# Routing scores of the last three token tiles on TensorE instead of VectorE

## The chip, the core and the metric

The kernel runs on one core of a Trainium2 chip. A core has five engines that run their instruction streams in order and wait for one another through semaphores: TensorE (PE, matmuls and transposes into PSUM), VectorE (DVE), ScalarE (ACT), GpSimd (POOL) and SyncE (SP, which issues most of the transfers). The metric is the time of one execution on the device in microseconds (us). Timed runs of the kernel before took 796.22, 793.3 and 797.24 us, median 796.22.

## What is computed

Attention over 4 x 8 heads of 576 tokens, then a dense layer with a maximum over three projections, then a layer of eight experts in which each of the 2304 tokens goes to one expert. The last part is the one that the change touches:

```python
logits = x @ w_gate + modality_bias[modality_id]      # 2304 x 512 by 512 x 8
e_idx = np.argmax(logits, axis=1)
probs = np.exp(logits - logits.max(-1, keepdims=True))
probs /= probs.sum(-1, keepdims=True) + 1e-09
gate_w = probs[np.arange(N), e_idx]
for e in range(8):
    mask = e_idx == e
    h = np.maximum(x[mask] @ w1[e], 0.0)              # 512 -> 1024
    out[mask] = gate_w[mask, None] * (h @ w2[e])      # 1024 -> 512
```

All is float32 outside. Inside, most matmuls take each operand as a high and a low part (`h`/`l`, `hh`/`hl`, `e_h`/`e_l`), three matmuls for one product.

## The kernel before, in words

Attention fills the first 287 us or so. Then come six windows of 384 tokens, three token tiles of 128 each, 18 tiles in all (t = 0 to 17). For a window, `stage_a` makes the six blocks of the hidden layer, and for each tile `stage_b` makes 18 matmuls (L528 to L530, "b") into `b_ps`; ACT copies the sum to `x2` (L532), SP writes it to `x2d` (L533), and `route` finds the expert of each token of the tile.

`route` before: eight products with sums on DVE (L459), one per expert, each over 512 elements of the tile against gate weights that are held broadcast over the 128 partitions (`wg_sb`, four buffers of the pool `raw2`); the bias (L460), the maximum, the one-hot of the first maximum (L451 to L453); on PE two matmuls that give each token its rank within its expert (L467, L468, one PSUM bank `rk`); on ACT the exponential (L473); and a scatter of token number and weight into the table in DRAM (L482, issued by POOL).

Experts are worked in units of up to 256 tokens of one expert. Three units (0, 1, 2) are cut from the first 12 tiles and start before the routing is done; the other units are found by arithmetic on DVE over the final counts (L706 to L758, "the table arithmetic") after tile 17. For a unit, POOL gathers the rows of x2 (`xg`), PE transposes them (L580, `x_ps`), ACT and DVE split them (L581, L582), `stage_1` is its first layer (96 matmuls L597 to L599 into `h_ps`; ACT makes `gh` at L600, DVE `gl` at L601) and `stage_2` its second (two halves of 24 matmuls, L626 to L628). Expert weights come in loads of 512 KB (`e_raw`, L563); ACT casts each half of a load to `e_h` (L567), and DVE (first half) or POOL (second half) subtracts to `e_l` (L568).

Loads need a raw buffer: unit 0's eight loads alternate between the two buffers of `rawp`; from the ninth load (unit 1) on they alternate between `rawp` and the four buffers of `raw2`. The casts need buffers that dense-layer weights held until the last b matmuls read them. All of this is one program; a scheduler orders the instructions of each engine by its own estimate, so that an edit can shift the order of work that it does not name. Small PSUM tiles come from `ps_a` (five banks in rotation), `x2`-sized tiles in SBUF from `x2p` (three buffers).

Of the kernel before, what the change touches and what calls it, by code (L numbers as in the profile page):

```python
# [5 lines left out]
F32 = mybir.dt.float32  # L6
# [3 lines left out]
ALU = mybir.AluOpType  # L10
# [7 lines left out]
DM = H * D  # L18
FF1 = 768
NF1 = FF1 // 128  # L20
E, FF2 = 8, 1024
# [18 lines left out]
MW = 384  # L40
NW = T // MW
NT = T // 128
# [3 lines left out]
STRIDE = T + UNIT  # L46
T_EARLY = NT - 2 * (MW // 128)
N_EARLY = 3
NU_STATIC = 6
NU_MAX = 16  # L50
SENT = 1 << 20
# [27 lines left out]
CONV = {2: [0, 1], 3: [2], 4: [3, 4], 5: [5], 7: [6], 8: [7], 9: [8]}  # L79


def fused_kernel(tc, qk, vd, sd, w64, mod, wg, mb, we, cst, csi, out):
    nc = tc.nc
    V, A, G, P, SP = nc.vector, nc.scalar, nc.gpsimd, nc.tensor, nc.sync
    top = ExitStack()
    with top:
# [13 lines left out]
        ident = per.tile([128, 128], F32, name="ident")  # L100
# [5 lines left out]
        bias = per.tile([128, NT, E], F32, name="bias")  # L106
# [38 lines left out]
        with ExitStack() as es:  # L145
# [249 lines left out]
            for p in range(1, NP):  # L395
# [17 lines left out]
                if p % (H // 2) == H // 2 - 1:  # L413
                    b = p // (H // 2)
                    n = 0
# [12 lines left out]
        x2p = top.enter_context(tc.tile_pool(name="x2p", bufs=3, reuse_waits="tile"))  # L428
# [5 lines left out]
        unp = top.enter_context(tc.tile_pool(name="unp", bufs=1, reuse_waits="tile"))  # L434
# [7 lines left out]

        junk = jkp.tile([128, DM], BF16, name="junk")
        wg_sb = []

        def first_max(src, mx):

# [7 lines left out]

        def route(t, x2):
            lg = rp.tile([128, E], F32, name="lg")
            for ei in range(E):
                V.tensor_tensor_reduce(out=junk, in0=x2, in1=wg_sb[ei // 2][:, ei % 2, :], scale=1.0, scalar=0.0, op0=ALU.mult, op1=ALU.add, accum_out=lg[:, ei:ei + 1])  # L459
            V.tensor_tensor(out=lg, in0=lg, in1=bias[:, t, :], op=ALU.add)  # L460
            nm = rp.tile([128, 1], F32, name="nm")
            mx = rp.tile([128, 1], F32, name="mx")
            V.tensor_reduce(out=mx, in_=lg, axis=AX.X, op=ALU.max)
            oh, _ = first_max(lg, mx)

            rk = ps_r.tile([128, E], F32, name="rk")
            P.matmul(rk, tri, oh, start=True, stop=False)  # L467
            P.matmul(rk, ones, acc[:, t, :], start=False, stop=True)  # L468
            V.tensor_tensor(out=acc[:, t + 1, :], in0=acc[:, t, :], in1=oh, op=ALU.add)
            V.tensor_scalar(out=nm, in0=mx, scalar1=-1.0, scalar2=None, op0=ALU.mult)  # L470
            ex = rp.tile([128, E], F32, name="ex")
            sm = rp.tile([128, 1], F32, name="sm")
            A.activation(out=ex, in_=lg, func=ACTF.Exp, bias=nm, scale=1.0, accum_out=sm)  # L473
            V.tensor_scalar(out=sm, in0=sm, scalar1=1e-9, scalar2=None, op0=ALU.add)
            V.reciprocal(out=meta[:, t, 1:2], in_=sm)
            sl = rp.tile([128, E], F32, name="sl")
            s1 = rp.tile([128, 1], F32, name="s1")
            V.tensor_tensor(out=sl, in0=rk, in1=off, op=ALU.add)
            V.tensor_tensor_reduce(out=sl, in0=sl, in1=oh, scale=1.0, scalar=0.0, op0=ALU.mult, op1=ALU.add, accum_out=s1)
            si = rp.tile([128, 1], I32, name="si")  # L480
            V.tensor_copy(out=si, in_=s1)
            G.indirect_dma_start(out=table[:, :], out_offset=bass.IndirectOffsetOnAxis(ap=si[:, 0:1], axis=0), in_=meta[:, t, :], in_offset=None, bounds_check=TABLE - 1, oob_is_err=False)  # L482
# [322 lines left out]
def _layout(i):  # L805
    import numpy as np

    def heads(a):
# [19 lines left out]
    csi = (np.arange(NT)[None, :] * 128 + np.arange(128)[:, None]).astype(np.int32)  # L828
    return {
        "qk": qk, "vd": vd, "sd": s, "w64": w64, "mod": mod,  # L830
        "wg": i["moe2_w_gate"].T.reshape(1, E, DM), "mb": i["moe2_modality_bias"].reshape(1, 2, E),
        "we": np.concatenate([e1, e2], axis=1), "cst": cst, "csi": csi,
    }

# [18 lines left out]
```

## Time and profile before

| | |
|---|---|
| median of three runs | 796.22 us (793.3 to 797.24) |
| the profiled execution | 794.2 us |
| its span, first to last instruction | 792.1 us |
| PE busy | 722.5 us, 91% |
| DVE busy | 580.4 us, 73% |
| POOL busy | 391.5 us, 49% |
| ACT busy | 360.7 us, 46% |
| mean granted clock of PE | 0.974 of full speed |

The trace gives every instruction its engine, its line in the kernel (L459), the tiles it writes and reads, its start and its length, all in us from the start of the span. Idle time of an engine is put down to what released the instruction behind it. Matmuls overlap, so PE's busy time says that it is fed, and the distance from one matmul's start to the next says how fast it goes.

### The profile page before, as it was taken

The page shows a single profiled execution, that of the slowest core. Times are in us where ns is not written, and L with a number is a line of the kernel's source. Part 1 is how long each engine was busy: PE and PEld are TensorE (multiplying, and loading weights), DVE is VectorE, ACT ScalarE, POOL GpSimd, SP SyncE. Part 2 cuts the span into 40 slices and gives each one's busy share as a digit, 9 for nine tenths or more (in the row PEclk, how much of TensorE's full clock was granted, in tenths as well). Part 3 has the DMA queues.
Part 4 walks back from the last instruction along what each step waited for, and adds up shares of the span by engine and source line. Part 5 has one row for each costly group of instructions (what it writes and reads, how often), then busy time and mean ns, then how long its engine had stood idle before and what let it go on. Part 6 is the DMA issues. An engine that isn't in the chain of part 4 may idle for free. (4 is left out here: it accounts for less than half of the span.)

```text
span 792.1 us, 13768 instructions
## 1 busy us (share of the span) xinstructions
PE 722.5 (91%) x4530; PEld 640.3 (81%) x4530; DVE 580.4 (73%) x1523; ACT 360.7 (46%) x905; POOL 391.5 (49%) x413
## 2 busy tenths in 40 slices
PE   2687789988999995999999999989988999999996
PEld 1565678767989785999989899988877899998884
DVE  4687897869867657867889495994997687657740
ACT  3364556544656544422222221333364755656541
POOL 6544546453342044645253423357375876857640
PEclk9988999998999999999999999999999999999998
DMA  7977778788672145210120101336375867657520
GB/s 192 214 219 205 193 198 206 194 220 215 193 177 82 42 167 193 103 62 21 51 47 15 37 14 32 125 81 165 108 226 205 300 224 255 242 196 255 184 83 18
DMA packets 50561, 117.99 MB, mean 149 GB/s; under 512 B 10352, under 2 KB 14352, under 8 KB 50480
## 3 DMA queue, kind: packets, MB, share of 16 engines
q1 hardware_dynamic: 38072, 90.44, 37.2%
q0 software_dynamic: 12400, 26.57, 13.0%
q8 instruction: 38, 0.62, 0.4%
q14 instruction: 43, 0.35, 0.1%
q10 hardware_dynamic: 8, 0.01, 0.0%
HBM read 98.84 MB, written 12.18 MB: 140 GB/s over the span
## 5 line engine op out<-in xcount | busy, mean ns | idle before, releaser
L139 PE MATMUL a_ps<-xh,w_h 128*128 128x384 f32 (+2 forms) x492 | 159.9, 326 | 3.6 <-DVE h L318 3.0
L140 PE MATMUL a_ps<-xl,w_h 128*128 128x384 f32 (+2 forms) x492 | 159.6, 325 | 0.0
L141 PE MATMUL a_ps<-xh,w_l 128*128 128x384 f32 (+2 forms) x492 | 158.1, 322 | 0.0
L459 DVE CUSTOM_DVE_ANT_0 junk<-x,wg 128x512 bf16<-128x512 f32 x144 | 114.3, 794 | 36.5 <-ACT x L532 34.8
L241 ACT ACTIVATE e<-e,mn 128x64 f32<-128x64 f32 (+4 forms) x160 | 89.1, 558 | 84.1 <-DVE mn L239 83.7
L568 DVE TENSOR_TENSOR e_l<-e_raw,e_h 128x512 fp32r<-128x512 f32 x80 | 103.6, 1307 | 32.3 <-ACT e_h L567 29.2
L568 POOL TENSOR_TENSOR e_l<-e_raw,e_h 128x512 fp32r<-128x512 f32 x80 | 109.3, 1385 | 32.1 <-ACT e_h L567 26.0
L567 ACT CAST e_h<-e_raw 128x512 fp32r<-128x512 f32 x160 | 93.7, 621 | 52.5 <-DMA e_raw<-in_we 42.9
L139 PEld LDWEIGHTS a_ps<-xh,w_h 128*128 128x128 f32 x492 | 93.6, 191 | 5.6 <-DVE h L318 3.8
L140 PEld LDWEIGHTS a_ps<-xl,w_h 128*128 128x128 f32 x492 | 93.9, 191 | 0.9
L141 PEld LDWEIGHTS a_ps<-xh,w_l 128*128 128x128 f32 x492 | 93.7, 191 | 0.5
L237 PE MATMUL s_ps<-hl 128*128 128x64 f32 (+2 forms) x192 | 67.4, 363 | 23.4 <-DMA hl<-in_qk 10.4
L270 PE MATMUL t_ps<-ident,e 128*128 128x128 f32 x480 | 73.8, 290 | 9.1 <-DVE x L295 4.5
L598 PE MATMUL h_ps<-x2t,e_h 128*128 128x256 f32 x288 | 81.2, 283 | 0.0
L599 PE MATMUL h_ps<-x2t,e_l 128*128 128x256 f32 x288 | 80.9, 282 | 0.0
L597 PE MATMUL h_ps<-x2t,e_h 128*128 128x256 f32 x288 | 80.4, 284 | 0.3 <-DVE gl L601 0.3
L519 POOL TENSOR_TENSOR fl<-h,fh 128x384 fp32r<-128x384 f32 x36 | 42.9, 1197 | 73.8 <-ACT fh L518 55.4
L270 PEld LDWEIGHTS t_ps<-ident,e 128*128 128x128 f32 x480 | 59.8, 149 | 13.2 <-DVE x L295 4.9
L239 DVE CUSTOM_DVE_ANT_0 e<-s_ps,mask 128x64 f32<-128x64 f32 (+4 forms) x160 | 64.3, 424 | 8.1 <-PE s_ps L238 7.3
L238 PE MATMUL s_ps<-k_b,q_b 66*128 66x64 f32 (+2 forms) x192 | 61.0, 329 | 4.6 <-POOL q_b L209 4.6
L628 PE MATMUL y_ps<-e_h,gl 128*128 128x512 f32 x152 | 61.3, 403 | 3.0 <-DVE gl L601 3.0
L237 PEld LDWEIGHTS s_ps<-hl 128*128 128x128 f32 x192 | 39.7, 209 | 29.7 <-DVE mn L239 13.4
(174 smaller groups left out, 1576.7 us busy)
## 6 DMA issues: line engine op xcount, KB each, us to landing
e_raw<-in_we SPq DMA_DIRECT2D x80, 512.0 KB
w_raw<-in_w SPq DMA_DIRECT2D x24, 512.0 KB
qk_r<-in_qk SPq DMA_DIRECT2D x32, 288.0 KB
hl<-in_qk POOLq DMA_DIRECT2D x32, 288.0 KB, 4.9
v_r<-in_vd SPq DMA_DIRECT2D x16, 320.0 KB
rb<-r_d SPq DMA_DIRECT2D x32, 160.0 KB
hl<-in_qk POOLq DMA_DIRECT2D x32, 144.0 KB, 4.0
x2d<-x SPq DMA_DIRECT2D x18, 256.0 KB
```

The lines of the kernel that those rows point to most:

```text
L139: P.matmul(a_ps, wh[:, c], xh[:, c], start=c == 0, stop=False)
L140: P.matmul(a_ps, wh[:, c], xl[:, c], start=False, stop=False)
L141: P.matmul(a_ps, wl[:, c], xh[:, c], start=False, stop=c == 3)
L237: P.matmul(s_ps, hl[:, 1, q0:q0 + nq], hl[:, 0, k0:k0 + n], start=True, stop=False)
L241: ex = A.activation(out=ec, in_=ec, func=ACTF.Exp, bias=mn[0:nq, c:c + 1], scale=-1.0, accum_out=l[0:nq, c:c + 1]).ins
L270: last_t[0] = P.transpose(out=t_ps[:, n * 128:(n + 1) * 128], in_=e[:, EOFF[c] + kb * 128:EOFF[c] + (kb + 1) * 128], identity=ident).ins
L459: V.tensor_tensor_reduce(out=junk, in0=x2, in1=wg_sb[ei // 2][:, ei % 2, :], scale=1.0, scalar=0.0, op0=ALU.mult, op1=ALU.add, accum_out=l ...
L567: A.copy(out=h, in_=raw[:, a])
L568: (G if a else V).tensor_tensor(out=lo, in0=raw[:, a], in1=h.bitcast(F32), op=ALU.subtract)
L597: P.matmul(h_ps, w(hs, f, c), xt[:, 0, c], start=c == 0, stop=False)
L598: P.matmul(h_ps, w(hs, f, c), xt[:, 1, c], start=False, stop=False)
L599: P.matmul(h_ps, w(ls, f, c), xt[:, 0, c], start=False, stop=c == 3)
```

## The change

The gate weights are loaded a second time, in the layout that PE needs (`wgt`, 128 partitions of 4 x 8). For the last three tiles (`T_PE` is 15) `route` transposes x2 in four pieces on PE, ACT copies the result from PSUM, and four float32 matmuls of 8 columns give the scores in PSUM, which the addition of the bias reads there. Tiles 0 to 14 are routed as before.

```diff
+T_PE = NT - MW // 128
...
+        wgt_sb = unp.tile([128, 4, E], F32, name="wgt")
+        SP.dma_start(out=wgt_sb, in_=wgt)
...
             lg = rp.tile([128, E], F32, name="lg")
-            for ei in range(E):
+            src = lg
+            if t >= T_PE:
+
+                t_ps = ps_a.tile([128, 512], F32, tag="a", name="xt_ps")
+                for c in range(4):
+                    P.transpose(out=t_ps[:, c * 128:(c + 1) * 128], in_=x2[:, c * 128:(c + 1) * 128], identity=ident)
+                x2t = x2p.tile([128, DM], F32, tag="x2", name="x2t_r").rearrange("p (c n) -> p c n", c=4)
+                A.copy(out=x2t, in_=t_ps.rearrange("p (c n) -> p c n", c=4))
+                src = ps_a.tile([128, 512], F32, tag="a", name="lg_ps")[:, 0:E]
+                for c in range(4):
+                    P.matmul(src, x2t[:, c], wgt_sb[:, c], start=c == 0, stop=c == 3)
+            for ei in range(E if t < T_PE else 0):
                 V.tensor_tensor_reduce(out=junk, in0=x2, in1=wg_sb[ei // 2][:, ei % 2, :], scale=1.0, scalar=0.0, op0=ALU.mult, op1=ALU.add, accum_out=lg[:, ei:ei + 1])
-            V.tensor_tensor(out=lg, in0=lg, in1=bias[:, t, :], op=ALU.add)
+            V.tensor_tensor(out=lg, in0=src, in1=bias[:, t, :], op=ALU.add)
```

Up to the end of tile 15's matmuls the order on the engines is the old one, but for the load of `wgt`. From there on it moves. On PE before, from the end of tile 16's matmuls on; `x_ps` are unit 0's input transposes, the 18 matmuls of tile 17 begin with the row L528, and L597 opens unit 0's first layer:

```order
L580 MATMUL x_ps<-ident,xg 128x128 x2
L530 MATMUL b_ps<-w_h,fl_6275 128x512 x2
L580 MATMUL x_ps<-ident,xg 128x128 x6
L528 MATMUL b_ps<-w_h,fh_6039 128x512
...
L530 MATMUL b_ps<-w_h,fl_6275 128x512
L597 MATMUL h_ps<-x2t,e_h 128x256 x3
```

And now, with the lines of the changed kernel (L543 to L545 are b, L467 the new transposes, x_6395, x_6459 and x_6538 tiles 15, 16 and 17, L472 the new scores, L595 unit 0's transposes, L482 and L483 the ranks, L612 unit 0's first layer):

```order
L545 MATMUL b_ps<-w_h,fl_6277 128x512 x2
L467 MATMUL xt_ps<-ident,x_6395 128x128 x4
L543 MATMUL b_ps<-w_h,fh_6041 128x512
...
L545 MATMUL b_ps<-w_h,fl_6277 128x512
L472 MATMUL lg_ps<-wgt,x2t_r 128x8 x4
L467 MATMUL xt_ps<-ident,x_6459 128x128 x4
L472 MATMUL lg_ps<-wgt,x2t_r 128x8 x4
L595 MATMUL x_ps<-ident,xg 128x128 x8
L467 MATMUL xt_ps<-ident,x_6538 128x128 x4
...
L483 MATMUL rk<-acc,ones 128x8
L472 MATMUL lg_ps<-wgt,x2t_r 128x8 x4
L612 MATMUL h_ps<-x2t,e_h 128x256
```

Routing of all three tiles and unit 0's transposes moved between tile 17's matmuls and unit 0's first layer. On ACT before, from the copy of tile 15 on (L581 casts unit 0's transposed input, L600 is gh):

```order
L532 COPY x_6393<-b_ps 128x512
L532 COPY x_6453<-b_ps 128x512
L581 CAST x2t<-x_ps 128x512 x2
L567 CAST e_h<-e_raw 128x512
L532 COPY x_6528<-b_ps 128x512
L600 ACTIVATE gh<-h_ps 128x256 x4
```

And now (L547 copies x2, L469 the transposed x2, L582 is e_h, L488 the exponential, L596 unit 0's input):

```order
L547 COPY x_6395<-b_ps 128x512
L469 COPY x2t_r<-xt_ps 128x512
L547 COPY x_6459<-b_ps 128x512
L582 CAST e_h<-e_raw 128x512 x6
L469 COPY x2t_r<-xt_ps 128x512
L547 COPY x_6538<-b_ps 128x512
L488 ACTIVATE ex,sm<-lg,nm 128x8
L596 CAST x2t<-x_ps 128x512
L488 ACTIVATE ex,sm<-lg,nm 128x8
L596 CAST x2t<-x_ps 128x512
L469 COPY x2t_r<-xt_ps 128x512
```

Five more casts of expert weights stand ahead of the copy of the transposed tile 16. On SP before, the last three writes of x2 stood ahead of the tenth expert load:

```order
L563 DMA e_raw<-in_we 128x1024
L533 DMA x2d<-x_6393 128x512
L533 DMA x2d<-x_6453 128x512
L533 DMA x2d<-x_6528 128x512
L563 ISA
```

And now three more loads stand ahead of the first two of them (L548), and four behind those ahead of the third:

```order
L578 ISA
L578 DMA e_raw<-in_we 128x1024
L548 DMA x2d<-x_6395 128x512
L548 DMA x2d<-x_6459 128x512
L578 ISA
```

The loads moved ahead because the gate weights' buffers are free after tile 14.

## Rows read from the trace of the kernel before

**Rows 1.** Page, busy time: us, share of the span, instructions.
```profile
PE 722.5 (91%) x4530; PEld 640.3 (81%) x4530; DVE 580.4 (73%) x1523; ACT 360.7 (46%) x905; POOL 391.5 (49%) x413
```

**Rows 2.** PE by stage: stage, length, PE busy (count), granted clock, DMA share, GB/s.
```profile
551.38:562.74 11.36, 11.36 (x99) 1.00 0.17 57
562.74:574.73 11.99, 11.99 (x60) 1.00 0.62 194
574.73:590.80 16.07, 13.22 (x100) 0.89 0.80 249
590.80:608.20 17.40, 14.44 (x58) 0.90 0.39 138
608.20:620.50 12.30, 12.02 (x97) 1.00 0.87 323
```

**Rows 3.** Waits of PE, 551 to 610: total us, times, longest.
```profile
PE y_ps L628 <- DVE gl L601: 3.0, 3, 1.4
PE rk L467 <- DVE sm L474: 2.7, 1, 2.7
```

**Rows 4.** Timeline of PE, 574 to 584: start us, length us, instruction.
```profile
577.19 0.27 PE L599 MATMUL h_ps<-x2t,e_l 128*128 128x256 f32 x1
...
580.19 0.56 PE L597 MATMUL h_ps<-x2t,e_h 128*128 128x256 f32 x1
...
583.11 0.35 PE L599 MATMUL h_ps<-x2t,e_l 128*128 128x256 f32 x1
```

**Rows 5.** Lines of DVE, 545 to 575: busy us, mean ns; idle before.
```profile
L459 DVE CUSTOM_DVE_ANT_0 junk<-x,wg 128x512 bf16<-128x512 f32 x24 | 17.7, 739 | 4.5 <-ACT x L532 4.2
L459 DVE DVE_READ_ACCUMULATOR2_ANT lg<- 128x1 f32 x24 | 2.0, 82 | 0.0
```

**Rows 6.** Timelines of DVE and POOL, 571 to 599.
```profile
571.45 2.87 DVE L460 TENSOR_TENSOR lg<-lg,bias 128x8 f32<-128x8 f32 x1
...
598.10 0.41 DVE L601 SCALAR_TENSOR_TENSOR gl<-h_ps,gh 128x256 fp32r<-128x256 f32 x1
...
571.75 2.54 POOL L568 TENSOR_TENSOR e_l<-e_raw,e_h 128x512 fp32r<-128x512 f32 x2
...
596.54 2.78 POOL L568 TENSOR_TENSOR e_l<-e_raw,e_h 128x512 fp32r<-128x512 f32 x2 [2.34 <-DMA e_raw<-in_we]
```

**Rows 7.** Timeline of SP, 530 to 610: issues, merged, with their count.
```profile
532.30 3.33 SPq L563 DMA_DIRECT2D e_raw<-in_we  x2
547.14 5.37 SPq L533 DMA_DIRECT2D x2d<-x  x3
565.39 32.34 SPq L563 DMA_DIRECT2D e_raw<-in_we  x15
```

**Rows 8.** Transposes and float32 matmuls: two timeline rows, two groups of lines.
```profile
777.57 1.03 PE L616 MATMUL t_ps<-ident,h 128*128 128x128 f32 x8
...
287.04 0.29 PE L293 MATMUL t_ps<-pt,v_r 128*64 128x64 f32 x4
...
L293 PE MATMUL o_ps<-pt,v_r 128*64 128x512 f32 x64 | 18.2, 647 | 2.2 <-ACT pt L275 2.2
...
L293 PE MATMUL t_ps<-pt,v_r 128*64 128x64 f32 x64 | 4.6, 222 | 0.0
```

**Rows 9.** Timeline of ACT, 536 to 549.
```profile
536.35 0.62 ACT L567 CAST e_h<-e_raw 128x512 fp32r<-128x512 f32 x1 [2.50 <-DMA e_raw<-in_we]
...
541.61 0.62 ACT L567 CAST e_h<-e_raw 128x512 fp32r<-128x512 f32 x1 [3.73 <-DMA e_raw<-in_we]
...
546.53 1.08 ACT L532 COPY x<-b_ps 128x512 f32<-128x512 f32 x2 [3.89 <-PE b_ps L530]
547.49 1.10 ACT L581 CAST x2t<-x_ps 128x512 fp32r<-128x512 f32 x2
```

**Rows 10.** Timeline of DVE: two of the small routing operations.
```profile
564.61 0.15 DVE L463 TENSOR_REDUCE mx<-lg 128x1 f32<-128x8 f32 x1
...
565.28 0.23 DVE L451 TENSOR_SCALAR lt<-lg,mx 128x8 f32<-128x8 f32 x1
```

More of the change, by code (lines that the diff above doesn't have):

```diff
@@ L79, with fused_kernel @@
 CONV = {2: [0, 1], 3: [2], 4: [3, 4], 5: [5], 7: [6], 8: [7], 9: [8]}
-def fused_kernel(tc, qk, vd, sd, w64, mod, wg, mb, we, cst, csi, out):
+def fused_kernel(tc, qk, vd, sd, w64, mod, wg, wgt, mb, we, cst, csi, out):
     nc = tc.nc
@@ L830, in _layout @@
         "qk": qk, "vd": vd, "sd": s, "w64": w64, "mod": mod,
-        "wg": i["moe2_w_gate"].T.reshape(1, E, DM), "mb": i["moe2_modality_bias"].reshape(1, 2, E),
+        "wg": i["moe2_w_gate"].T.reshape(1, E, DM), "wgt": i["moe2_w_gate"].reshape(4, 128, E).transpose(1, 0, 2), "mb": i["moe2_modality_bias"].reshape(1, 2, E),
         "we": np.concatenate([e1, e2], axis=1), "cst": cst, "csi": csi,
```

## Prediction

> **What bounds the kernel now.** I first read the busy table of the page [rows 1]: TensorE (PE) is busy for 91% of the span. Then I cut the end of the program into stages and read PE in each [rows 2]: the two layers of unit 0 (551.38 to 562.74 and to 574.73) are busy throughout, 11.36 and 11.99 us. The same two layers of unit 1 take 16.07 and 17.40 us, at a granted clock of 0.89 and 0.90 on the mean. So PE loses 4.71 + 5.41 = 10.1 us there, and unit 2's first layer 12.30 - 11.36 = 0.9 us more. The reader is to see that PE sets the time, and that its large holes behind the routing lie between 574.7 and 608.2.
>
> Third, who makes the holes: the waits of PE [rows 3] name DVE alone, 2.7 us before a rank matmul (the last token tile's) and three times before L628 (3.0 us). The timeline [rows 4] shows the first: nothing from 577.46 to 580.14, and behind it 13 steps from matmul to matmul in 2.92 us where such steps take 11.36/96 = 0.118 us each, 1.5 in all: 1.4 us more, at the lower clock level of 1.2 GHz after an idle stretch. DVE is late because it works off 24 products (17.7 us, and 2.0 us for reading their sums [rows 5]), and because single small operations of it stretch to 2.87 us while POOL subtracts [rows 6].
>
> Fourth, the load queue [rows 7]: SP issues the last write of x2 at about 552, and its next item only at 565.39, then 15 expert loads in a row. The first of these needs a buffer that the gate weights hold until DVE's products are through.
>
> **What the change removes.** 24 products and 24 reads, 19.7 us of DVE between 547.1 and 570.8. In that stretch itself they hide no PE time: PE is full there [rows 2]. Their price is paid behind it: the 2.7 us wait, the clock after it, the lag of gl before L628, and loads that come 13 us late. If all of that goes, 10.1 us go.
>
> **What it adds on PE.** Per tile 4 transposes and 4 small float32 matmuls. Eight transposes of this size took 1.03 us [rows 8]: 0.13 us each, 0.52 per tile. No row shows a float32 matmul of 8 columns on 128 weights. From below it is a transpose, 0.13 us; from above the float32 matmul of 512 columns, 0.65 us; nearest is the 64-column one, 0.22 us [rows 8]. I take 0.22: 0.9 us per tile (bounds 0.52 and 2.6). With the transposes 1.4 us per tile, 4.3 us in all if PE never waited (3.1 to 9.4).
>
> FP8 and Floating Point Precision (the Trainium skill, TensorE Precision Notes) says that true float32 makes four passes through the array. Were each pass to cost what a transpose costs [rows 8], an estimate is 0.52 us per small matmul, 3.6 us more over the twelve; by that the sum below would come to +3.4 instead of -0.2 us. The trace shows four float32 matmuls of 64 columns done 0.29 us after the first began [rows 8], which speaks against so much.
>
> **What it moves.** The order on PE is the larger term. Before, unit 0's eight input transposes stood ahead of the last tile's 18 matmuls (b), and unit 0's first layer followed them directly, at 551.38. Now all of the routing of the three tiles, and those eight transposes, stand between the last b and unit 0's first layer, and PE takes them in order, each waiting for ACT or DVE. I follow it through:
> - ACT's copy of tile 15 ends at 547.07 (half of the pair [rows 9]); its four transposes take 0.52, so b ends at 551.9 instead of 551.4.
> - Scores of 15: 0.9 us, to 552.8; transposes of 16 to 553.3.
> - ACT has six casts e_h ahead of the copy of the transposed tile 16. The sixth takes the buffer that the last b matmul frees at 551.9, so it ends at 552.6 (0.62 us [rows 9]). The copy then waits for the transposes only: to 553.85 (0.55 us, half of the pair L581 [rows 9]); scores of 16 to 554.8.
> - Unit 0's eight transposes (1.03) to 555.8; transposes of 17 to 556.3.
> - DVE: six dependent small operations of 0.15 to 0.23 us [rows 10] and a subtraction of about 0.7 make the one-hot of 15 at 554.3; that of 16 from 554.9 on, to 556.1. There is one rank bank, so the rank of 16 waits until DVE has read that of 15: 557.0.
> - ACT: copy of x 17, two exponentials, two casts, copy of the transposed 17: to 557.7; scores of 17 to 558.6. Unit 0's layer could start.
> - One or two of the DVE steps will meet a POOL subtraction, three of which stand together on POOL there: 1.3 us. Start at 559.9.
>
> That is 8.5 us after 551.38. Its lower bound is what PE itself has to do in between: scores 2.7, transposes of 16 and 17 1.04, unit 0's eight 1.03, ranks 0.3, the later end of b 0.5, 5.6 us; the upper bound is rival C. PE has gaps there of the kind that dropped its clock at 580, so I charge the same 1.4 us once.
>
> SBUF — State Buffer (the Trainium skill, SBUF: two separate sides) says that DVE and GpSimd share a port pair under an exclusive lock, which a DVE operation with two SBUF inputs needs against a GpSimd operation that reads SBUF. The rows agree: the addition of scores and bias ended at 574.32, with POOL's pair of subtractions at 574.29, while gl, which reads PSUM, took its 0.41 us beside POOL [rows 6]. The changed addition reads the scores from PSUM, so by that rule it would not stretch, and the 1.3 us of the last step above might fall away.
>
> The gate weights' second copy is one more SP item of 16 KB ahead of the end of attention, where SP is not what PE waits for: at nothing, and an issue of a fraction of a microsecond if that cover is gone. The writes of x2 of 15 and 16 now stand on SP behind three expert loads that no longer wait for the gate weights (the tenth to the twelfth), and ACT may refill their buffers only when they are written: the basis of rival C. The earlier loads thin out the rush of 574.7 to 590.8, where the DMA share was 0.80 [rows 2].
>
> **The sum.** From unit 0's first layer to unit 2's PE needs 11.36 + 11.99 twice, 46.7 us, if nothing holds it; before it took 56.8. Starting 8.5 us later and with 1.4 us for the clock: -10.1 + 8.5 + 1.4 = -0.2 us. Behind 608.2 the work is the same in both. The profiled execution took 794.2 us (span 792.1 and 2.1 around it), 2.0 below the median of 796.22; the runs reach from 793.3 to 797.24. On the scale of the median that is 796.0; I take 0.5 off for the 0.9 us of unit 2, which earlier loads may give back: 795.5, no change that can be told.
>
> **Rivals.**
> B. Clearly faster: the chain costs no more than PE's own work (5.6 us late, no drop of the clock), and unit 2's 0.9 us come back too: -10.1 - 0.9 + 5.6 = -5.4, 791 us. For it: DVE is free from 547 on, and loads come early. Against it: every handover between four in-order engines must be prompt.
> C. Slower, by transfers in ACT's queue: the copy of the transposed tile 16 stands behind a cast that needs the twelfth load, and behind the write of x2. Two loads landed 4.0 and 6.3 us after issue (issues at 532.3 and 535.3 [rows 7], casts that waited for them at 536.35 and 541.61 [rows 9]). Three more at 6 us one after another from 541.6 end at 559.6, the write of x2 at 562.6, and unit 0 starts at 569 instead of 559.9: +9, 805 us. It decides from a start later than 561.5 on, where the 10.1 us are used up. Against it: 57 GB/s were moved from 551.4 to 562.7 [rows 2], so the queue has room.
> D. The stalls before L628 stay, since the table arithmetic and POOL's subtractions make them and not the products: only the 4.7 us of the first layer come back, and -4.7 + 8.5 + 1.4 = +5, 801 us. For it: DVE was through with the products over 20 us before those waits. Against it: in the new order the table falls into unit 0's first layer, and the last gl is needed only 5 us into the second.
>
> **How the numbers follow.** Forecast 0.57 (own range 792.5 to 799), B 0.20, C 0.08, D 0.15. The range from 789.5 to 802 holds the forecast, most of B, and D; C and the far end of B are left out. Half a per cent (4 us) is about what a measurement of this kernel can tell from no change: faster 0.20 (B), slower 0.21 (C and most of D), same 0.59.
>
> **What would show it.** In the profile after: unit 0's first layer starts between 558 and 561.5; PE has gaps from 552 to 560 ahead of the scores of 16 and 17, ended by ACT; unit 1's layers take under 12.5 us each; SP shows no stretch of 13 us without a load; DVE is some 19 us less busy. Wrong would be a start before 556 or after 562, 3 us of waits before L628's counterpart as before, or a rank matmul of tile 17 that still waits 2 us.

## The result, and the profile after

The changed kernel takes 798.79 us, median of 22 runs (796.51 to 803.8). The kernel before took 794.55 us in 22 runs beside it (789.63 to 800.35). The ratio is 1.0053, 95% interval 1.0033 to 1.0072: it is slower by 4.2 us (2.6 to 5.7). The time lies inside the range that was given. But the forecast was no change, and half a per cent slower is a change.

The page's busy line, which answers to [rows 1]:

```profile
PE 726.9 (91%) x4566; PEld 644.7 (80%) x4566; DVE 558.4 (70%) x1475; ACT 361.7 (45%) x908; POOL 388.5 (48%) x413
```

DVE is 22 us less busy and PE 4.4 us more, as intended, and the time still went up. This profiled execution took 803.8 us, 5 more than the median. The part ahead of the routing, which is the same in both kernels but for one small load, ran later in it: the last matmul of attention began at 291.93 (before at 287.10), the last b matmul ended at 556.06 (before at 551.54, 4.5 us earlier). Whether that belongs to the change is tested below; so stages are compared by their lengths, not by their clock times.

The stages of the changed kernel, by windows (stage, length, PE busy and count, PEld, DVE, ACT and POOL the same way, granted clock, DMA share, GB/s). The first runs from tile 17's second b matmul to unit 0's first layer, the others answer to the five of [rows 2]:

```profile
551.99:563.46 11.47, 8.85 (x63) 7.78 (x61) 9.08 (x33) 7.78 (x17) 7.44 (x6) 1.00 0.83 277
563.46:576.72 13.26, 13.26 (x102) 13.18 (x102) 9.09 (x29) 5.14 (x13) 5.72 (x6) 0.87 0.18 46
576.72:589.54 12.82, 12.11 (x59) 9.80 (x57) 10.25 (x23) 6.73 (x14) 6.92 (x6) 1.00 0.51 158
589.54:606.82 17.28, 14.33 (x98) 14.06 (x97) 10.41 (x22) 7.81 (x17) 5.41 (x5) 0.80 0.44 156
606.82:618.92 12.10, 12.10 (x59) 9.78 (x58) 4.83 (x7) 5.52 (x11) 10.61 (x9) 1.00 0.66 217
618.92:630.42 11.50, 11.50 (x97) 11.50 (x96) 8.49 (x12) 8.66 (x19) 7.41 (x6) 1.00 0.81 293
```

Read it against [rows 2] line by line:

- Unit 0's first layer starts 7.4 us after the last b matmul's end (556.06). Before, it started with it. That is +7.6 us.
- Unit 0's two layers take 13.26 and 12.82 us instead of 11.36 and 11.99: +1.9 and +0.8.
- Unit 1's first layer takes 17.28 instead of 16.07: +1.2, where 4.7 less was forecast.
- Unit 1's second layer takes 12.10 instead of 17.40, unit 2's first 11.50 instead of 12.30: -5.3 and -0.8.

The sum is +5.4 us from the last b matmul to unit 2's second layer; from there on TensorE works back to back in both. What holds up unit 1's first layer is told by the waits of PE (total us, times, longest us; 545 to 635):

```profile
PE h_ps L613 <- DVE x2t L597: 2.9, 1, 2.9
PE rk L482 <- DVE sl L493: 1.9, 1, 1.9
PE lg_ps L472 <- ACT x2t_r L469: 0.7, 1, 0.7
PE y_ps L641 <- ACT gh L615: 0.7, 1, 0.7
PE xt_ps L467 <- ACT x L547: 0.5, 1, 0.5
```

The waits of unit 1's second layer and of the last rank [rows 3] are gone. In their place there is one at the second matmul of unit 1's first layer, for x2t, the low part of that unit's transposed input, which DVE writes. DVE's timeline shows why it is late (start us, length us, instruction):

```profile
572.02 0.16 DVE L722 TENSOR_TENSOR cn<-cn,took 128x8 f32<-128x8 f32 x1
...
573.62 3.12 DVE L734 TENSOR_TENSOR nu<-cn,full 128x8 f32<-128x8 f32 x1
...
581.34 1.29 DVE L583 TENSOR_TENSOR e_l<-e_raw,e_h 128x512 fp32r<-128x512 f32 x2 [2.47 <-ACT e_h L582]
...
586.79 3.10 DVE L761 TENSOR_TENSOR st<-un,st 128x17 f32<-128x17 f32 x1
...
591.94 0.18 DVE L772 TENSOR_SCALAR ut<-at 128x17 int32<-128x17 f32 x1
592.02 1.28 DVE L597 TENSOR_TENSOR x2t<-x_ps,x2t 128x512 fp32r<-128x512 f32 x2
```

The whole table arithmetic (L722 to L772) stands on DVE ahead of x2t. It is 28 operations, and it lasts from 572 to 592, because DVE also waits for a cast and because single operations stretch to 3 us. POOL's timeline shows what they stretch beside:

```profile
574.16 2.55 POOL L583 TENSOR_TENSOR e_l<-e_raw,e_h 128x512 fp32r<-128x512 f32 x2
...
587.31 2.54 POOL L583 TENSOR_TENSOR e_l<-e_raw,e_h 128x512 fp32r<-128x512 f32 x2
```

The pairs end together: 576.74 and 576.71, 589.89 and 589.85. PE's timeline at the wait:

```profile
589.54 0.28 PE L612 MATMUL h_ps<-x2t,e_h 128*128 128x256 f32 x1
592.77 0.58 PE L613 MATMUL h_ps<-x2t,e_h 128*128 128x256 f32 x1 [2.95 <-DVE x2t L597]
593.14 0.41 PE L614 MATMUL h_ps<-x2t,e_l 128*128 128x256 f32 x1
593.36 0.41 PE L612 MATMUL h_ps<-x2t,e_h 128*128 128x256 f32 x1
```

Behind the wait matmuls follow each other at 0.22 us instead of 0.118: the lower clock level again, 0.80 on the mean of that layer. The wait (2.95 us) and the slower matmuls behind it (28 steps, until 598.8) make the 5.9 us that the layer takes over 11.36.

### The profile page after: what moved, and what is told of

It is laid out like the page before. It is cut to its first block, busy times and chain, and to the rows that moved or that the text cites. A ratio compares the mean times of both kernels' runs of the same rounds, so it can differ in the third digit from the quotient of the medians.

```text
span 802.0 us, 13814 instructions
## 1 busy us (share of the span) xinstructions
PE 726.9 (91%) x4566; PEld 644.7 (80%) x4566; DVE 558.4 (70%) x1475; ACT 361.7 (45%) x908; POOL 388.5 (48%) x413
## 5 line engine op out<-in xcount | busy, mean ns | idle before, releaser
L583 DVE TENSOR_TENSOR e_l<-e_raw,e_h 128x512 fp32r<-128x512 f32 x80 | 101.9, 1288 | 43.2 <-ACT e_h L582 35.3
L474 DVE CUSTOM_DVE_ANT_0 junk<-x,wg 128x512 bf16<-128x512 f32 x120 | 96.6, 805 | 32.0 <-ACT x L547 30.6
L582 ACT CAST e_h<-e_raw 128x512 fp32r<-128x512 f32 x160 | 92.6, 621 | 43.3 <-DMA e_raw<-in_we 36.3
L613 PE MATMUL h_ps<-x2t,e_h 128*128 128x256 f32 x288 | 83.0, 289 | 2.9 <-DVE x2t L597 2.9
L614 PE MATMUL h_ps<-x2t,e_l 128*128 128x256 f32 x288 | 82.7, 288 | 0.0
L612 PE MATMUL h_ps<-x2t,e_h 128*128 128x256 f32 x288 | 81.9, 288 | 0.0
L641 PE MATMUL y_ps<-e_h,gh 128*128 128x512 f32 x152 | 61.6, 405 | 1.1 <-ACT gh L615 0.7
```

The lines of the kernel that those rows point to most:

```text
L582: A.copy(out=h, in_=raw[:, a])
L583: (G if a else V).tensor_tensor(out=lo, in0=raw[:, a], in1=h.bitcast(F32), op=ALU.subtract)
L612: P.matmul(h_ps, w(hs, f, c), xt[:, 0, c], start=c == 0, stop=False)
L613: P.matmul(h_ps, w(hs, f, c), xt[:, 1, c], start=False, stop=False)
L614: P.matmul(h_ps, w(ls, f, c), xt[:, 0, c], start=False, stop=c == 3)
```

## The experiments

Two theories were set against each other first. W: the loss lies behind the routing, in the later start of unit 0 and in the new wait of unit 1. S: the added load disturbs attention, and the shift of 4.5 us is the loss. (The 541.9 and 537.6 of the first expectation below are the starts of one of the last matmuls of the hidden layer, not of attention.)

**The changed kernel again**, as it is.

> The changed kernel once more, as the yardstick for the runs beside it. Every theory expects what was measured first, a ratio of 1.005 to the kernel before (1.003 to 1.007). The profiled execution tells how much of the 4.4 us by which the attention part of the first profile was later (last product of its third quarter at 274.4 instead of 269.6, last of the whole at 541.9 instead of 537.6) belongs to the kernel: theory S (the added load of the gate weights disturbs attention) expects the last attention matmul at 541 to 543 again, theory W (the loss lies behind the routing, the shift is chance of one execution) one anywhere from 535 to 543.

Measured: 802.27 us, ratio 1.0083 (1.0061 to 1.0105). Its last b matmul ended at 549.88, 6.2 us earlier than in the first profile of the same kernel. So the shift is a matter of the execution and not of the kernel. From that matmul to unit 2's second layer it took 74.95 us (74.36 in the first profile, 68.95 before). The waits of PE there:

```profile
PE h_ps L613 <- DVE x2t L597: 4.1, 1, 4.1
PE y_ps L641 <- ACT gh L615: 3.0, 1, 3.0
```

**Only the load** is added to the kernel before: `T_PE = NT`, so that no tile's scores go to TensorE.

> Only the second load of the gate weights is added to the kernel before; all scores stay on DVE. Theory S (the added load costs the 4.4 us seen in attention): 1.005. Theory W (the loss lies behind the routing): 1.000, within 0.2%, about 794.5 us.

Measured: 793.99 us, 0.9975 (0.9952 to 0.9998). The added load costs nothing that can be told; S falls.

**The table arithmetic later.** The block from the counts of all tiles to the unit table moves behind the first pass of the loop over units:

```
-        U, NK, X = NU_MAX, T // UNIT, 2 * E      # to ut: ahead of the loop
...
             if nxt and nxt["n"] > 128:
                 stage_1(nxt)
+            if n == 0:
+                U, NK, X = NU_MAX, T // UNIT, 2 * E      # to ut
```

> The changed kernel with the table arithmetic (the lines from the counts of all tiles to the unit table) moved behind unit 1's layers, so that on DVE nothing of it stands ahead of unit 1's input. Theory W (unit 1's first layer took 17.2 us instead of 11.4 because its input stands on DVE behind that arithmetic: 2.95 us of wait, and the lower clock after it): that layer takes 11.4 to 12.5 us, 5 us come back, 793.5 us, ratio 0.997 to 1.000. Rival L (late expert loads, raw buffers freed late by POOL, hold that layer): PE then waits at the same place for the casts of the weights, ratio stays at 1.003 to 1.006. Theory S: stays at 1.005.

Measured: 796.99 us, 1.0018 (0.9994 to 1.0042), against 1.0083 for the changed kernel in the same comparison. Unit 1's first layer, by windows (columns as above):

```profile
588.08:599.35 11.27, 11.27 (x98) 11.23 (x97) 8.95 (x12) 7.17 (x16) 7.48 (x6) 1.00 0.61 213
```

11.27 us with nothing waited for and at the full clock: with the arithmetic moved, those 5.9 us are gone, so its place ahead of x2t was their cause. PE did not wait for weights there either, so rival L falls. The end of W's range (1.000) lies inside the interval; in this profile unit 0's second layer waited 1.5 us for gh and ran 13.65 us.

**The last tile's routing later.** Unit 0's transposes go ahead of the last three tiles; its first layer, the last tile's routing and unit 1's transposes go ahead of the table arithmetic, in this order:

```
-            route(t, x2)
+            if t in LATE:
+                late.append((t, x2))
+            else:
+                route(t, x2)
...
+        early, late, LATE = [], [], (NT - 1,)
...
-                if w == NW - 1 and i == 2:
+                if w == NW - 1 and i == 0:
                     transposed(early[0])
...
+        u = early[0]
+        stage_1(u)
+        for t, x2 in late:
+            route(t, x2)
+        transposed(early[1])
         U, NK, X = NU_MAX, T // UNIT, 2 * E
...
```

> The changed kernel in another order: unit 0's input transposes stand ahead of the last three tiles, unit 0's first layer and unit 1's transposes ahead of the routing of the last tile and of the table arithmetic. Theory W with the chain (7.7 us until unit 0's layer starts, 5.9 us in unit 1's first layer): unit 0's layer starts some 4 us after the last b matmul, unit 1's first layer takes under 12.5 us, 8 to 9 us less than the changed kernel: 790 us, ratio 0.993 to 0.996. Theory S: 4.4 us more of it, 0.998 to 1.001. Rival L: unit 1's layers start earlier and wait for weights instead, 1.000 to 1.004.

Measured: 791.81 us, 0.9943 (0.9920 to 0.9966), as W said. The stages from the last b matmul's end on, by windows:

```profile
556.25:559.16 2.91, 2.19 (x21) 1.95 (x20) 2.91 (x1) 1.49 (x3) 2.78 (x3) 1.00 0.63 177
559.16:570.96 11.80, 11.80 (x102) 11.71 (x102) 9.11 (x39) 5.31 (x15) 2.44 (x3) 1.00 0.62 201
570.96:584.22 13.26, 13.26 (x72) 11.14 (x71) 9.00 (x18) 9.60 (x19) 10.77 (x9) 1.00 0.55 186
584.22:595.88 11.66, 11.63 (x98) 11.52 (x97) 11.35 (x33) 6.27 (x14) 6.81 (x7) 1.00 0.46 175
595.88:607.96 12.08, 12.08 (x59) 9.77 (x57) 7.33 (x19) 5.27 (x11) 6.53 (x6) 1.00 0.40 139
607.96:619.76 11.80, 11.76 (x97) 11.56 (x96) 10.97 (x10) 7.67 (x18) 9.37 (x8) 1.00 0.92 308
```

PE waits 0.7 us in the first and is full from then on at the full clock. Unit 0 starts 2.9 us after the last b matmul instead of 7.4. Part of that is only moved: ahead of the last b matmul PE now waits for the gathered rows that unit 0's transposes read:

```profile
PE x_ps L598 <- DMA xg<-x2d,mt: 1.1, 1, 1.1
```

From the last hidden-layer matmul to the end of the last b matmul it takes 16.33 us here, 13.57 before and 13.78 in the changed kernel. By the medians this version beats both kernels.

The next runs ask where the pieces of that come from.

**The kernel before with the table arithmetic later**, the same move without the change.

> The kernel before with only the table arithmetic moved behind unit 1's layers; all scores stay on DVE. Theory D (the table arithmetic, not the products, makes the waits in unit 1's second layer): the 5.4 us of that layer and the 0.9 us of unit 2 come back, the 4.7 us of unit 1's first layer (rank wait behind the products) stay: 789 us, ratio 0.991 to 0.994. Theory P (the products leave DVE so late that gl lags whatever stands behind them): 0.998 to 1.001.

Measured: 798.65 us, 1.0051 (1.0019 to 1.0083), slower than both theories gave. Its waits of PE:

```profile
PE h_ps L598 <- DVE x2t L582: 3.9, 1, 3.9
PE rk L467 <- DVE sm L474: 3.0, 1, 3.0
PE y_ps L628 <- DVE gl L601: 0.7, 1, 0.7
```

The waits of unit 1's second layer fall from 3.0 us to 0.7, as D had it. But the arithmetic now stands ahead of unit 2's input, and the same kind of wait (3.9 us, and 18.02 us for that layer at a clock of 0.81) appears there. With the products still on DVE, neither of the two places tried for the block is free: the wait moves. A further 3.7 us are lost behind unit 2 (171.56 us from its second layer to the end before, 175.23 here). In unit 3's first layer one subtraction on DVE stands beside five of POOL's:

```profile
635.00 7.52 DVE L568 TENSOR_TENSOR e_l<-e_raw,e_h 128x512 fp32r<-128x512 f32 x1 [0.51 <-ACT e_h L567]
635.71 6.25 POOL L568 TENSOR_TENSOR e_l<-e_raw,e_h 128x512 fp32r<-128x512 f32 x5
```

It takes 7.52 us, where such a subtraction takes 0.69 elsewhere. gl stands behind it, PE waits 2.0 us for gl, and the layer takes 15.02 us instead of 11.20. In the kernel before a subtraction at that place took 6.13 us, and PE waited for nothing.

**Unit 0's transposes early**, only the first of the three moves (`i == 0`).

> The changed kernel with unit 0's input transposes put ahead of the last three tiles again, as they stood before; nothing else moves. Theory W with the chain: 1.0 us of PE leaves the stretch between the last b matmul and unit 0's first layer, which starts 6 to 6.6 us after it instead of 7.6; unit 1's first layer is as slow as in the changed kernel (about 17 us): ratio 1.004 to 1.006. Rival (the ranks and one-hots of DVE alone set the start): 7.6 us as before, 1.005 to 1.008.

Measured: 803.41 us, 1.0108 (1.0059 to 1.0156). Unit 0 starts 6.7 us after the last b matmul instead of 7.4, and unit 1's first layer still takes 17.2 us, both near the expectation; the time is above what W gave (to 1.006), and in any case no better, so this move alone is not the gain. The 0.7 us are paid ahead: PE waits 0.8 us there for unit 0's gathered rows, and the way to the last b matmul takes 14.94 us instead of 13.78.

**Routing late and the table arithmetic late**, both; unit 1's transposes stay where the changed kernel has them.

> The order with the last tile's routing behind unit 0's first layer, and the table arithmetic also behind unit 1's layers. Theory W: unit 0's and unit 1's layers then run at 11.4 to 12.2 us each, unit 0's starts 3 us after the last b matmul, some 51 us from there to unit 2's first layer: 790 to 791 us, 0.993 to 0.995, no better than the same order with the table arithmetic ahead, since DVE was not waited for there. Rival L (weights and transfers hold those layers): 0.996 to 1.000.

Measured: 792.03 us, 0.9960 (0.9926 to 0.9995): no better than with the table arithmetic ahead, as expected.

**One tile** on TensorE: `T_PE = NT - 1`.

> Only the last tile's scores go to TensorE, those of the two before stay on DVE. Chain theory: 1.4 us of added PE work instead of 4.3 and one hand-over instead of three, unit 0's first layer 3.0 us after the last b matmul; of the 11 us that the kernel before loses to waits in units 1 and 2, 6 to 11 come back: 788 to 792 us, 0.990 to 0.995. Rival (the gate weights still hold the raw buffers for 16 products, loads come late, and the waits of unit 1 stay): 1.000 to 1.004.

Measured: 799.11 us, 1.0043 (1.0004 to 1.0081); the rival's side. The waits of PE begin with

```profile
PE lg_ps L472 <- ACT x2t_r L469: 4.6, 1, 4.6
PE h_ps L612 <- DVE gl L616: 3.5, 2, 2.0
```

The copy of the transposed tile takes the buffer that x2 of tile 15 held. DVE's products read that x2 until 554.81, and the profile names its write as what ended last; the copy ran at 556.29, and unit 0 started 7.6 us after the last b matmul with one hand-over, as with three. This is rival C's kind of wait, by another buffer.

**e_l off POOL**, to test the stretched operations. Unit 1's eight subtractions that POOL did go to DVE too:

```
-                    (G if a else V).tensor_tensor(out=lo, in0=raw[:, a], ...
+                    (G if a and n != 1 else V).tensor_tensor(out=lo, in0=raw[:, a], ...
```

> The changed kernel, with the eight subtractions e_l of unit 1's two layers that POOL did now on DVE too (8 times 0.69 us more DVE work). Unit 1's input still stands on DVE behind the table arithmetic. Theory K (single small DVE operations stretch to 3 us while POOL subtracts, and that alone makes the table arithmetic last until after unit 0's second layer): no operation of the table arithmetic takes over 0.6 us, the 3 to 4 us wait of unit 1's first layer falls under 1 us, 5 us less than the changed kernel, 0.997 to 1.001. Rival Q (there is simply too much in DVE's queue ahead of it): with 5.5 us more DVE work the wait grows to 6 us or more, 1.008 to 1.012.

Measured: 796.21 us, 0.9973 (0.9942 to 1.0004). With 5.5 us more work on DVE, the kernel got faster than the changed one; rival Q falls. K is shown in part only. The wait for x2t is 2.5 us, not under 1, although the first half of x2t now stands ahead of the last seven operations of the arithmetic. Unit 1's first layer is 3.0 us shorter than in the first profile of the changed kernel (14.33), but the wait gives only 0.4 of that; the rest is the clock, which stayed at 1.00 behind this wait and was 0.80 behind that one. The reason for the wait is on DVE's and POOL's timelines, where unit 2's subtractions had moved up:

```profile
582.91 3.23 DVE L763 TENSOR_TENSOR oh<-at,iota 128x289 f32<-128x289 f32 x1
...
586.40 1.19 DVE L764 TENSOR_TENSOR oh<-oh,row 128x289 f32<-128x289 f32 x1
587.52 1.23 DVE L761 TENSOR_TENSOR st<-un,st 128x17 f32<-128x17 f32 x1
```

```profile
583.26 5.45 POOL L583 TENSOR_TENSOR e_l<-e_raw,e_h 128x512 fp32r<-128x512 f32 x4
```

Three operations of the arithmetic filled POOL's 5.45 us; the second and third took 0.44 and 0.17 us in the kernel before with the table late.

**The same on the kernel before.**

> The kernel before with the same eight subtractions moved from POOL to DVE. Theory K: the waits of units 1 and 2 that cost 10 to 11 us come in part from the stretched operations, so 2 to 5 us come back: 790 to 793 us, 0.994 to 0.998. Theory P (the products leave DVE late, more work on DVE makes it later): 1.003 to 1.008.

Measured: 799.5 us, 1.0014 (0.9985 to 1.0043): no change that can be told, and the low end of P's range is inside the interval. The profile shows that again the hold moves: unit 1's first layer takes 11.49 us with no wait for the rank, but its second takes 20.8 (PE waits 5.3 us for gl at once; one small operation of the arithmetic takes 5.40 us beside four subtractions of POOL), and unit 3's first 16.39 behind a subtraction of 6.78 us.

**The new order with all scores on DVE.** Routing late as above, on the kernel before.

> The order that gave 0.994 with all scores on TensorE for the last three tiles, but with all scores on DVE as before: unit 1's transposes and the last tile's routing and the table arithmetic behind unit 0's first layer. If the order alone makes that gain (theory O): 4.3 us of PE work less than with scores on TensorE, 0.988 to 0.993. If the scores on TensorE are needed for it (theory N: the products keep DVE busy until 571 and hold the buffers of the loads, whatever the order behind them): unit 1's first layer waits 2 to 4 us for a rank or its input, 0.998 to 1.003.

Measured: 799.3 us, 1.0033 (1.0000 to 1.0066), on the side of N: the order alone doesn't give the gain. PE waits for a rank and for gl:

```profile
PE rk L467 <- DVE sm L474: 3.6, 1, 3.6
PE h_ps L600 <- DVE gl L604: 3.5, 2, 3.2
PE y_ps L631 <- DVE gl L604: 2.4, 1, 2.4
```

**The new order and e_l on DVE.**

> The order that gave 0.994, and unit 1's subtractions e_l on DVE. TensorE is nearly full there (1.1 us of gaps between unit 0's first layer and unit 2's), so theory K expects no more than 1 us of it: 0.992 to 0.995. Rival Q: DVE has 5.5 us more and unit 1's input or gl comes late, 0.998 to 1.002.

Measured: 793.57 us, 0.9959 (0.9931 to 0.9986): nothing more to gain there, as K said. The interval touches Q's range too, and DVE was late once: PE waits 2.2 us for gl in unit 2's first layer, which takes 15.49 us.

Four more runs ask for prices and bounds.

**Unit 1's input first.** Unit 0's first layer and unit 1's transposes are written ahead of the table arithmetic, the routing as in the changed kernel.

> The changed kernel with unit 1's input transposes and their low parts written ahead of the table arithmetic (unit 0's first layer too); POOL, the table arithmetic and the routing stay. Theory W: unit 1's first layer waits for nothing and takes 11.4 to 12.2 us instead of 17, ratio 0.998 to 1.002. If it were the stretch of all DVE work beside POOL and not the place of the input (rival K2): gl or the low part lag all the same, 3 us of wait, 1.003 to 1.006.

Measured: 798.99 us, 1.0024 (0.9993 to 1.0055). The interval holds W's range and most of K2's, so the time does not decide. The profiled execution was the longest of the twelve (803.95 us), so no difference in time is read from it, but it shows what PE waited for in unit 1's first layer (15.48 us):

```profile
PE h_ps L612 <- DVE gl L616: 2.4, 1, 2.4
```

The wait for x2t is gone: its halves are through at 586.33 and 588.50, ahead of most of the arithmetic. But the arithmetic now runs from 583.95 to 599.85, ahead of that layer's gl (600.38), and PE waits for gl. So moving the input alone does not free the layer, against W. It is the sign that K2 named, but it does not single out the stretch: the place of the block and its stretched operations (one of 2.82 us) both stand ahead of gl. How the wait divides between them stays open.

**The scores twice**, in the new order: `for c in [0, 1, 2, 3] * 2:` around the small matmul.

> The order with the last tile's routing late (0.994), each of the twelve small score matmuls issued twice: 12 more at 0.23 us, 2.8 us of TensorE work. If TensorE's own time is what the change costs there (theory T): +2.8 us, 0.9975 within 0.2%. If the handovers hide it (rival): 0.993 to 0.995.

Measured: 796.48 us, 1.0011 (0.9980 to 1.0042), 5.4 us over the new order, give or take 3.1 by both intervals. The added PE time is not hidden; 2.8 us, one for one, lies inside that. The profile shows where more may come from: the clock was 0.73 between the last b matmul and unit 0's layer and 0.87 in it, where the new order had 1.00.

**Two routings late**: tiles 16 and 17 behind unit 0's first layer.

> The same order, with the routing of the last two tiles behind unit 0's first layer. Theory W with the chain: that layer starts about 1 us after the last b matmul instead of 2.9, and the same PE work is done later; unit 1's layers see no wait if the scores of both tiles are through by then: 0.991 to 0.994. Rival: the table arithmetic comes 6 us later and meets unit 1's layers, or ranks wait on PE ahead of unit 1: 0.996 to 1.000.

Measured: 794.93 us, 0.9984 (0.9956 to 1.0012). Unit 0 starts 0.6 us after the last b matmul, but unit 1's first layer takes 15.7 us, at a clock of 0.89: ranks and the counts now stand on PE inside it. What is saved ahead is given back.

**One tile in the new order.**

> The same order with only the last tile's scores on TensorE. Theory N (the gate weights hold the buffers of the expert loads until DVE's products are through): the copy of the transposed tile no longer waits 4.6 us in front of unit 0, but unit 1's layers wait for gl or weights behind 16 products, 0.997 to 1.002. Rival O (PE work decides): 2.9 us less than with three tiles, 0.989 to 0.993.

Measured: 797.16 us, 1.0003 (0.9970 to 1.0036), N's side: a rank waits 4.8 us behind DVE.

All of them together. The stretch runs from the end of the last b matmul to the start of unit 2's second layer in the profiled execution. "Ahead" is the time from the last hidden-layer matmul to the end of the last b matmul, against 13.57 us before, and "behind" the time from unit 2's second layer to the last instruction, against 171.56. The times are of one profile, the ratios of medians of six to 22 runs, so 2 to 4 us apart is nothing:

```
kernel                        unit 0 starts  unit 1's 1st  stretch  against 68.95  ahead  behind  ratio to before
before                             -0.2          16.1       68.95        -            -      -           -
changed, first profile              7.4          17.3       74.36      +5.4         +0.2    0.0       1.0053
changed, again                      7.4          17.1       74.95      +6.0         +0.5   +0.2       1.0083
only the load                      -0.2          14.0       68.12      -0.8         +0.2   +0.8       0.9975
table arithmetic late               7.4          11.3       70.10      +1.2         +0.2   +0.3       1.0018
e_l on DVE                          6.4          14.3       68.39      -0.6         +0.3   +0.1       0.9973
unit 0's transposes early           6.7          17.2       74.17      +5.2         +1.4   +0.2       1.0108
unit 1's input first                7.4          15.5       73.94      +5.0         +0.6   +0.2       1.0024
new order                           2.9          11.7       63.51      -5.4         +2.8   +1.0       0.9943
new order, table late               2.9          11.3       65.49      -3.5         +1.9    0.0       0.9960
new order, e_l on DVE               2.9          11.6       67.01      -1.9         +1.8   +0.1       0.9959
new order, two routings             0.6          15.7       68.10      -0.9         +2.0    0.0       0.9984
new order, scores twice             6.3          11.6       70.09      +1.1         +2.0   +1.5       1.0011
new order, one tile                -0.2          11.6       72.86      +3.9          0.0   +0.1       1.0003
new order, scores on DVE           -0.2          16.6       72.84      +3.9          0.0   +1.7       1.0033
before, table late                 -0.2          14.5       69.87      +0.9          0.0   +3.7       1.0051
before, e_l on DVE                 -0.2          11.5       67.03      -1.9          0.0   +5.6       1.0014
one tile                            7.6          15.3       75.75      +6.8          0.0   +0.7       1.0043
```

(Columns: us from the last b matmul's end to unit 0's first layer; us of unit 1's first layer; the stretch in us; its difference; the differences ahead and behind.) Half a per cent is 4 us. The stretch and the ratio agree within 4 us in every row, which is no more than one profile can tell. The stretch is not the whole: the kernels of the new order that score three tiles on TensorE pay 1.8 to 2.8 us ahead of it, and the kernel before with the table late or with e_l on DVE loses 3.7 and 5.6 us behind it.

## Why the prediction was wrong

**The step that failed** is the one that credited what is removed: "If all of that goes, 10.1 us go". It counted unit 1's two layers at 11.36 and 11.99 us once the products had left DVE. The second came back as forecast (5.3 us of 5.4), and unit 2's 0.8 with it. The first did not: forecast 4.7 less, measured 1.2 more (17.28, and 17.14 in the second profile). That is 5.9 us, where the whole error of the sum is 5.6 and 6.2 (-0.2 forecast for the stretch, +5.4 and +6.0 measured). The other errors nearly cancel; among them is unit 0's second layer, for which the forecast had nothing: +0.8 in the first profile and +3.1, the largest of them, in the second ("Loads" below). The products were one hold on that layer; the table arithmetic was the next in DVE's order. Before, the counts that begin it came at 584.45, 32.9 us after the last b matmul, and it ran for the most part under unit 1's second layer. Now they come at 571.37, 15.3 us after that matmul, and it stands ahead of unit 1's input. The table-late run shows it: 11.27 us for the layer when nothing of the arithmetic stands ahead. The length of the block is in part due to a late load (a subtraction in it waits 2.47 us for a cast) and to operations that stretch beside POOL; how the 5.9 us divide between its place and its length is not shown.

Rival D had the suspect, the size (+5) and a chance of 0.15, but the wrong stage: it kept the stalls before L628, which went, and let the first layer come back, which didn't. Its own remark, that the table falls into unit 0's first layer in the new order, was the clue; it was not followed to the next thing on DVE. In the kernel before, though, D was right on the cause: with the table late, the waits in unit 1's second layer fell from 3.0 to 0.7 us.

**Unit 0's start**: 8.5 us later forecast, of which 0.5 is a later end of b; 7.6 measured in both profiles from the end of b, and 0.2 and 0.5 ahead of it. Right in kind and nearly in size. The waits on the way were 0.5 (the copy of x), 0.7 (the copy of the transposed tile 16) and 1.9 us (the rank bank, ahead of the rank of 16). The small matmuls of a tile took about 0.9 us, and the value taken per matmul, 0.22, fits:

```profile
L472 PE MATMUL lg_ps<-wgt,x2t_r 128*128 128x8 f32 x24 | 3.1, 254 | 0.7 <-ACT x2t_r L469 0.7
L467 PE MATMUL xt_ps<-ident,x 128*128 128x128 f32 x12 | 1.9, 280 | 0.5 <-ACT x L547 0.5
```

(Lines of PE from 545 to 570: the 24 records of twelve matmuls are busy 3.1 us, 0.26 each; twelve transposes 1.9, 0.16 each.) So the estimate of 0.52 us per matmul, worked out beside the rule of FP8 and Floating Point Precision (the Trainium skill, TensorE Precision Notes), is not what these rows show.

**The clock**: 1.4 us charged once. Unit 0's first layer lost 1.9 us in the first profile and 0.4 in the second; one charge was fair there. But unit 1's wait brought a second drop, which the forecast had not, since it had no wait there.

**The lock-out step** of 1.3 us came in size, but not in the operations that the forecast had in mind. POOL's three subtractions ran from 553.63 to 558.29. The sum of scores and bias of tile 15 took 0.15 us beside them, as long as elsewhere; what stretched were subtractions of DVE, also the one that stood behind that sum, ahead of the one-hot of 15 (0.69 us elsewhere, 1.48 here):

```profile
554.10 3.07 DVE L583 TENSOR_TENSOR e_l<-e_raw,e_h 128x512 fp32r<-128x512 f32 x2 [6.08 <-ACT e_h L582]
557.09 0.15 DVE L475 TENSOR_TENSOR lg<-lg_ps,bias 128x8 f32<-128x8 f32 x1
...
557.36 1.48 DVE L583 TENSOR_TENSOR e_l<-e_raw,e_h 128x512 fp32r<-128x512 f32 x1
```

SBUF — State Buffer (the Trainium skill, SBUF: two separate sides) would have it so: this addition has one input in PSUM, and the trace agrees. Two operations of tile 16 then stretched beside a POOL fill (0.94 and 0.80 us, shown in the last section; 0.22 and 0.14 for those of tile 15). All of this stands on DVE ahead of the read of the rank bank for which PE waited 1.9 us; an estimate from these lengths is 0.8 and 0.7 us, 1.5 in all. So the 1.3 us did not fall away, though the sum itself was not held. The same rule was read for this step only. Where it mattered was 15 us further on, in the arithmetic on SBUF alone.

**Loads**: "SP shows no stretch of 13 us without a load" is wrong. SP's timeline:

```profile
559.22 2.17 SPq L548 DMA_DIRECT2D x2d<-x  x1
575.50 24.45 SPq L578 DMA_DIRECT2D e_raw<-in_we  x8
```

14 us without an issue, and 16 without a load. Four loads went out early (554.96); the next one came while POOL's pair of subtractions ran (574.16 to 576.71), which are among the readers of the raw buffers. That these held it was not tried by itself. Unit 0's second layer paid for it (0.7 us of wait for gh, which stood on ACT behind a cast that waited 4.8 us for its load; 3.0 us in the second profile). **Rival C** at 0.08 did not occur with three tiles. **Rival B** was not reached either. That the new order's stretch has B's very figure, -5.4, is in part chance: it is another program, its terms differ (unit 0 starts 3.1 us later and its layers take 1.7 more, where B had 5.6 for the start), and it pays 2.8 us ahead of the stretch that B did not have. What it shows is that about as much is to be had by moving the routing: 4.5 us by the medians.

## What to carry to other kernels

When work is taken off an engine that runs in order, ask what stands next in its queue ahead of the operation that the bound engine waits for, and read that operation's length in the trace; a recovered stall counts only as far as the next hold. Work moved to the engine that sets the time is not hidden, and it brings hand-overs; here it gained only when the routing that it serves was also taken out of the way of the first layer. The order alone gained nothing (1.0033, interval from 1.0000), the change alone lost (1.0053), together they gained (0.9943). Moved work and moved waits also have to be looked for outside the stretch that one watches: several of the versions here paid 2 to 6 us ahead of it or behind it.

## What the runs showed of the hardware

- A DVE operation on 128x8 elements took 3.12 us beside a pair of POOL subtractions and ended with it, and such operations 0.15 to 0.17 us elsewhere. A DVE subtraction of 128x512 took 7.52 us beside five of POOL's in a row, and 0.69 us elsewhere. Not only operations with two SBUF inputs stretch: beside a POOL fill of 0.95 us (560.11 to 561.06) two small ones with a scalar operand did so, and ended at 561.08:

```profile
560.14 0.94 DVE L455 TENSOR_SCALAR lt<-lg,mx 128x8 f32<-128x8 f32 x1
560.28 0.80 DVE L485 TENSOR_SCALAR nm<-mx 128x1 f32<-128x1 f32 x1
```

- The same wait on PE does not always cost the same clock. After the 1.9 us wait for the rank bank, PE's clock fell to 0.52 for 3.5 us (564.70 to 568.20) in one profile of the changed kernel and not at all in the other. After unit 1's wait it was 0.80 on the mean of the layer after 2.95 us, 0.90 after 4.07.
- The end of the last b matmul lies between 546.75 and 556.38 us in these profiles, though the kernels differ ahead of it by 2.8 us at most ("ahead" in the table). In the two of the changed kernel the granted clock from 100 to 200 us was 0.93 and 1.00. One profile's time is therefore no measure of a change of 4 us. The stretch behind the last b matmul repeats better: 74.36 and 74.95 us in the two profiles of the changed kernel.
